# A softcap-attention and soft-MoE kernel on one core: one vector operation moved behind the norm in chunk 53, and matrix products without use put into two waits of TensorE

## The chip, the cores and the metric

The kernel runs on one core of a Trainium2 chip. The metric is the device time of one execution in microseconds (us). The core has five engines that run side by side, each with its own queue in program order: TensorE (PE in the profile, with its weight loads listed apart as PEld), VectorE (DVE), ScalarE (ACT), GpSimd (POOL) and SyncE (SP, which here only starts transfers). An engine waits on semaphores that other engines or transfers raise.

## The reference

Attention over 8 batches of 12 heads, 448 tokens of 64 values each, with capped scores, and then a soft mixture of experts over all 3584 tokens of 768 values, with 32 slots for 8 experts. Its core:

```python
scores = scale * q @ k.T;  scores = cap * tanh(scores / cap)
attn = softmax(scores);    x = (attn @ v)           # 3584 x 768
logits = x @ phi                                     # 3584 x 32
d = softmax(logits, over tokens); c = softmax(logits, over slots)
slot_input = d.T @ x                                 # 32 x 768
h = relu(slot_input[e] @ w1[e]); slot_out[e] = h @ w2[e]
out = c @ slot_out                                   # 3584 x 768, float32
```

## The kernel before, in words

**Tiles and chunks.** Heads are taken in 48 pairs, and the keys of a pair in 7 tiles, so there are 336 tiles of 128 x 448 scores. Six tiles are a chunk; there are 56 chunks (0 to 55). Two halves of a chunk have three tiles each. The main loop (lines 899 to 932) goes over the chunks j. In each round it issues, engine by engine in this order: the tanh of the chunk's two halves on ScalarE (`tanh_chunk`, line 354, its instructions are L361 and L365), the exponential of the chunk before on ScalarE (`exp_chunk`, line 375, L373), the product of finished exponentials with the values for the pair that ended two chunks ago (`pv_first`, line 654, `pv_tail`, line 667, `pv_rest`, line 671; the products are L634), and the scores of the next chunk (`qk_chunk`, line 337, L348).

**The exponential chain.** ScalarE does not take all exponentials. `SHARED` (line 381) gives VectorE the first 1 to 3 tiles of some chunks. `poly_exp` (line 603) computes them as a chain of seven operations, numbered 0 to 6 (L609, L611, L612, L613, L614, L615, L616); operations 2 to 5 work on two tiles of scratch, `xf` and `xp`, of which there is one each. The table `POLY` (line 382) says where in the round each operation of each chunk is issued: the key is a chunk and a slot, the slot's sign says whether it stands ahead of ("<") or behind (">") the other work of that slot.

**Slots.** `run(j, slot)` (line 866) issues the work that `at(j, slot, ...)` put there (line 795). Within a round the slots come in the order 0, m, e, a, b, r, c, d. Between slot b and slot c stands `pv_rest`, which ends with the norm.

**The norm.** `norm` (line 638) reads the sums of a pair from the PSUM tile `pv`, takes their reciprocal (L641) and multiplies (L644) into `xq`. There is one `pv` tile (pool `psV`, one buffer), so the next pair's first product waits until L644 has read it.

**Work around chunk 53.** In slot a of a round with a finished pair, `pv_first` writes `pv`; slot c of chunk 53 has `slot_sums` of batch 6 (line 778; L769, L775 and L727 on TensorE, L785 on VectorE). GpSimd copies values into `vbd` (`vcast`, line 285, L288) when the products that read it have ended.

**Products without use.** `busy` (line 878, L882 and L885) multiplies ones into a bank that nobody reads; `spare` (line 800) does it in the `pv` bank; `fill` (line 660, L664) multiplies ones into 57 unused columns of the last `pv` tile. `FILL` (line 804) and `LATE` (line 860) say where. In chunk 34 slot b has `e_transp` of batch 3 (line 730, L739), and slot c a `spare`.

**The start.** `first_half(0)` (line 240) prepares the first pair: casts, transposes on TensorE (L236), and copies (L238). The list at lines 249 to 255 is the order of its pieces. The transposes of key tiles 3 to 6 go into the bank `three`, a part of the tile `boots[1]`, and wait for GpSimd's cast of those keys (L232) and for ScalarE's copy out of `three`.

**After the chunks.** The last pairs are finished (`TAILSEQ`, line 999), the slot inputs are summed, and the two layers of the experts run on TensorE (L1078, L1106). Some parts of w2 come back from a scratch tensor by 21 transfers that SyncE starts as attention's memory is given back (L1057). Then output tiles are made and stored (L1134).

Of the kernel before, what the change touches and what calls it, by code (L numbers as in the profile page):

```python
# [20 lines left out]
NT = 7  # L21
# [3 lines left out]
CS = 3  # L25
# [12 lines left out]
def kernel(  # L38
# [31 lines left out]
    pe, dve, act, pool, sp = nc.tensor, nc.vector, nc.scalar, nc.gpsimd, nc.sync  # L70
# [111 lines left out]
    def load(nm, Q):  # L182
        if Q < NQ:
            t = raw_tile(nm)
            pool.dma_start(out=t, in_=quad_ap(nm, Q))  # L185
            raws[nm, Q] = t
# [37 lines left out]
    def first_pieces(h, jobs):  # L224

        for stage, nm, c0, c1, eng, bank, at0 in jobs:
            copy = act.copy if eng is act else pool.tensor_copy if eng is pool else dve.tensor_copy
            cols = slice(h * HP, h * HP + HP)
            if stage == "junk":
                busy(c0)  # L230
            elif stage == "cast":
                copy(casts[nm, 0][:, c0:c1, cols],  # L232
                     raws[nm, 0][h][:, c0 * DH:c1 * DH].rearrange("p (c d) -> p c d", d=DH))
            elif stage == "turn":
                for c in range(c0, c1):
                    pe.transpose(bank[cols, at0 + c - c0, :], casts[nm, 0][:, c, cols], ident)  # L236
            else:
                copy(qkT[nm, 0][cols, c0:c1, :], bank[cols, at0:at0 + c1 - c0, :])  # L238

    def first_half(h):  # L240
        for nm in ("k", "q"):
            if h == 0:
                qkT[nm, 0] = qk[0].tile([P, NT, P], BF16, name=nm + "T", tag=nm + "T")
        one = psT.tile([P, 8, P], BF16, name="ps1", tag="T")
        two = psV.tile([P, NT, P], BF16, name="ps2", tag="pv")
        if h == 0:

            three = boots[1][:, CS - 1, :].bitcast(BF16).rearrange("p (c q) -> p c q", q=P)
            first_pieces(h, (("cast", "q", 4, NT, act, None, 0), ("cast", "k", 0, CS, dve, None, 0),
                             ("cast", "q", 0, 4, dve, None, 0), ("turn", "q", 4, NT, pe, three, 0),  # L250
                             ("turn", "k", 0, CS, pe, two, 0), ("copy", "q", 4, NT, act, three, 0),
                             ("cast", "k", CS, NT, pool, None, 0),
                             ("turn", "q", 0, 4, pe, one, 0), ("copy", "k", 0, CS, dve, two, 0),
                             ("copy", "q", 0, 4, dve, one, 0), ("turn", "k", CS, NT, pe, three, 3),
                             ("copy", "k", CS, NT, dve, three, 3)))
        else:
            first_pieces(h, (("cast", "k", 0, NT, dve, None, 0), ("cast", "q", 0, NT, dve, None, 0),
                             ("turn", "k", 0, NT, pe, two, 0), ("turn", "q", 0, NT, pe, one, 0),
                             ("copy", "k", 0, NT, dve, two, 0), ("copy", "q", 0, NT, dve, one, 0)))
            for nm in ("q", "k"):  # L260
                raws.pop((nm, 0)), casts.pop((nm, 0))
                load(nm, 2)
# [112 lines left out]
    def exp_chunk(j):  # L375
# [201 lines left out]
            (53, 'm'): ((52, 2),),  # L577
            (53, 'e'): ((53, 0), (52, 3), (51, 6), (52, 4)),
            (53, '>a'): ((53, 1), (52, 5)),
            (53, '<b'): ((53, 2),),  # L580
            (53, '>d'): ((53, 3),),
            (54, 'm'): ((54, 0),),
            (54, 'e'): ((53, 4), (52, 6)),
# [211 lines left out]
    def at(j, slot, f, *a):  # L795
        if j < 0:
            j, slot = 0, "b"
        aux.setdefault((j, slot), []).append((f, a))
# [61 lines left out]
    LATE = ((52, 'd', 3, 1), (54, 'd', 3, 3),)  # L860
    for j, slot, n, parts in LATE:
        at(j, slot, spare, n, parts)
    for n in range(2):
        at(0, "c", vcast, 0, n)

# [10 lines left out]
    junk = boots[0][:, 0, 0:P]  # L876
# [11 lines left out]
    junk = boots[1][:, 0, 0:P]  # L888
    busy(27)
    first_half(0)  # L890
    qk_chunk(0)
    qk_chunk(1)
    spare(6)
    first_half(1)
    pool.dma_start(out=phib, in_=moe_phi.rearrange("(jt ji) s -> ji jt s", ji=P))

# [62 lines left out]
    junk = sl_ps[1][:, P:512]  # L959
# [220 lines left out]
    for n in range(B // 2 * NT):  # L1180
        bb, c = divmod(n, NT)
# [58 lines left out]
```

## Time and profile before

| what | us |
|---|---|
| three runs: median (lowest to highest) | 286.31 (284.74 to 288.71) |
| the profiled execution: device time | 283.64 |
| the profiled execution: span of its instructions | 281.9 |
| PE busy in the span | 245.5 (87%) |
| ACT busy | 249.2 (88%) |
| DVE busy | 240.0 (85%) |
| POOL busy | 141.4 (50%) |

Busy time is a union over the engine's instructions and says how full an engine is, not whether anything waits for it. The lines that are used are quoted where they are used. Times in the timeline and in the chain of waits are counted from the start of the span.

### The profile page before, as it was taken

How to read it: one execution, taken by the hardware profiler on the slowest of the kernel's cores; microseconds unless marked ns; L12 is line 12 of the kernel's file. 1: busy time of each engine (PE TensorE's matmuls, PEld its weight loads, DVE VectorE, ACT ScalarE, POOL GpSimd, SP SyncE). 2: the span in 40 equal slices, each digit the busy share in tenths (PEclk: the TensorE clock that was granted, in tenths of full speed). 3: DMA queues.
4: the chain of work that ended last, by engine and by line, in shares of the span. 5: the costliest groups of instructions: out<-in, count | busy, mean ns of one | idle time of the engine just before them, and what ended most of it. 6: DMA issues, size and time to landing. Idle time of an engine off the chain costs nothing.

```text
span 281.9 us, 10429 instructions
## 1 busy us (share of the span) xinstructions
PE 245.5 (87%) x4553; PEld 165.9 (59%) x4553; DVE 240.0 (85%) x474; ACT 249.2 (88%) x198; POOL 141.4 (50%) x198
## 2 busy tenths in 40 slices
PE   8898889998998999889989999899988989997720
PEld 6655556765675667566657675667566758642400
DVE  3479999999999999999999999999999996447840
ACT  4999999999999999999999999999999996236730
POOL 7986457653955385628663857295734210200000
PEclk9999999999999999999999999999999999999985
DMA  7999999999999999999999999999999579959997
GB/s 228 266 192 204 224 212 229 232 221 218 211 225 222 216 230 231 219 216 218 230 219 203 212 225 223 217 214 226 221 217 218 137 226 318 410 200 391 414 420 306
DMA packets 58332, 68.08 MB, mean 242 GB/s; under 512 B 4144, under 2 KB 54448, under 8 KB 58288
## 3 DMA queue, kind: packets, MB, share of 16 engines
q0 software_dynamic: 42448, 35.31, 79.5%
q1 hardware_dynamic: 15552, 31.89, 32.4%
q8 instruction: 35, 0.57, 0.7%
q10 hardware_dynamic: 288, 0.23, 0.2%
q14 instruction: 9, 0.07, 0.1%
HBM read 91.72 MB, written 19.27 MB: 394 GB/s over the span
## 4 chain that ended last, share of the span: by engine, by line
ACT 40%; PE 29%; DVE 20%; issue 4%; DMA 3%; POOL 1%; DVEq 0%; ACTq 0%; POOLq 0%
ACT ex L373 16%; ACT ex L365 15%; PE pv L634 8%; ACT ex L361 7%; PE sc L348 4%; DVE xq L644 3%; DVE xp L612 3%; PE so_ps L1106 2%; DVE xp L614 2%; PE hp L1078 2%; DVE xf L611 2%; DVE qT L280 2%; DVE ex L609 2%; DVE ex L615 2%; PE op L1146 1%
## 5 line engine op out<-in xcount | busy, mean ns | idle before, releaser
L365 ACT ACTIVATE ex<-sc 128x1344 f16<-128x1344 f32 (+1 forms) x91 | 118.2, 1400 | 1.3 <-PE sc L348 1.3
L373 ACT ACTIVATE ex<-ex 128x1344 bf16<-128x1344 f16 (+5 forms) x58 | 109.7, 1894 | 0.1
L634 PE MATMUL pv<-vbd,ex 128*128 128x130 bf16 (+1 forms) x1610 | 95.1, 212 | 10.2 <-POOL vbd L288 4.4
L634 PEld LDWEIGHTS <-ex 128*128 128x128 bf16 (+1 forms) x1680 | 75.6, 101 | 38.8 <-issue 6.2
L288 POOL CAST vbd<-vraw 64x896 bf16<-64x896 f32 x46 | 47.8, 1040 | 58.4 <-PE pv L634 40.1
L348 PE MATMUL sc<-qT,kT 64*64 64x448 bf16 x672 | 66.5, 359 | 5.3 <-ACT ex L365 3.7
L348 PEld LDWEIGHTS <-kT 64*64 64x64 bf16 x672 | 22.4, 105 | 14.4 <-ACT ex L365 6.3
L644 DVE TENSOR_TENSOR xq<-pv,rec 128x448 bf16<-128x448 f32 x46 | 28.7, 624 | 1.6
L361 ACT ACTIVATE ex<-sc 128x2688 f16<-128x2688 f32 x11 | 28.1, 2550 | 0.2 <-PE sc L348 0.2
L614 DVE TENSOR_TENSOR xp<-xp,xf 128x1344 f16<-128x1344 f16 (+2 forms) x34 | 27.4, 807 | 0.5
L612 DVE TENSOR_TENSOR xp<-xf 128x1344 f16<-128x1344 uint16 (+2 forms) x34 | 27.5, 809 | 0.2
L615 DVE TENSOR_TENSOR ex<-ex,xp 128x1344 uint16<-128x1344 uint16 (+2 forms) x34 | 26.9, 791 | 0.2
L116 POOL DMA_DIRECT2D w1b<-in_moe_w_dram x32 | 25.9, 810 | 0.0
L280 DVE COPY kT<-kps 128x896 bf16<-128x896 bf16 x23 | 14.2, 616 | 4.9 <-PE kps L275 2.8
L609 DVE TENSOR_SCALAR ex<-ex 128x1344 uint16<-128x1344 f16 (+2 forms) x34 | 17.0, 501 | 1.2 <-ACT ex L361 0.7
L296 POOL MEMSET vbd<- 64x1 bf16 x22 | 3.1, 139 | 29.3 <-PE pv L634 29.0
L613 DVE TENSOR_SCALAR xp<-xp 128x1344 f16<-128x1344 f16 (+2 forms) x34 | 17.2, 506 | 0.6
L611 DVE TENSOR_SCALAR xf<-ex 128x1344 uint16<-128x1344 uint16 (+2 forms) x34 | 17.1, 504 | 0.3
L185 POOL DMA_DIRECT2D qb<-in_q_dram x22 | 16.3, 740 | 1.8 <-PE qps L278 0.9
L616 DVE TENSOR_SCALAR ex<-ex 128x1344 uint16<-128x1344 uint16 (+2 forms) x34 | 16.1, 474 | 0.2
L185 POOL DMA_DIRECT2D kb<-in_k_dram x22 | 16.3, 741 | 0.0
L120 POOL DMA_DIRECT2D w2d<-in_moe_w_dram x21 | 16.1, 785 | 0.0
(124 smaller groups left out, 317.8 us busy)
## 6 DMA issues: line engine op xcount, KB each, us to landing
w1b<-in_moe_w_dram POOLq DMA_DIRECT2D x32, 384.0 KB, 9.8
vraw<-in_v_dram SPq DMA_DIRECT2D x44, 224.0 KB, 6.2
w2d<-in_moe_w_dram POOLq DMA_DIRECT2D x21, 384.0 KB, 9.0
w2t<-w2d SPq DMA_DIRECT2D x21, 384.0 KB, 7.4
out_dram<-ob SPq DMA_DIRECT2D x7, 768.0 KB, 6.9
qb<-in_q_dram POOLq DMA_DIRECT2D x22, 224.0 KB, 8.0
kb<-in_k_dram POOLq DMA_DIRECT2D x22, 224.0 KB, 7.7
w2b<-in_moe_w_dram POOLq DMA_DIRECT2D x11, 384.0 KB, 9.0
```

The lines of the kernel that those rows point to most:

```text
L116: pool.dma_start(out=w1b[e][:, js, fs], in_=w1r[:, e, js, fs])
L185: pool.dma_start(out=t, in_=quad_ap(nm, Q))
L288: pool.tensor_copy(vbds[Q % 2][r, :, :, c0:c0 + DH], raw[r])
L348: ins = pe.matmul(sc[cs, u, 0:S], qkT["k", Q][r, c, cs], qkT["q", Q][r, :, cs], start=True, stop=True).ins
L361: apart["t", i - 1] = apart["t", i] = act.activation(exs[j].bitcast(F16), own["board"][:, :, 0:S], ACT.Tanh, scale=qk_scale / cap).ins
L365: ins = act.activation(exs[j][:, half * CS + u0:half * CS + u1, :].bitcast(F16), (own[0] if i == u0 == 0 else sc)[:, u0:u1, 0:S], ACT.Tanh ...
L373: act.activation(exs[j][:, u0:u1, :], exs[j][:, u0:u1, :].bitcast(F16), ACT.Exp, scale=cap)
L612: lambda: dve.tensor_tensor(p, s, s.bitcast(F16), op=ALU.mult),
L614: lambda: dve.tensor_tensor(p, p, s, op=ALU.mult),
L615: lambda: dve.tensor_tensor(y, y, p, op=ALU.add),
L634: pe.matmul(out_, exs[j][r, u, q0:q0 + (HP if tail else P)], v_, start=(c == 0 and g == gs[0] < NF), stop=(c == NT - 1), skip_group_check= ...
L644: dve.tensor_tensor(xq[Q][:, h, s0:s1, :], pv[:, 0:s1 - s0, 0:DH], rec.to_broadcast([P, s1 - s0, DH]), op=ALU.mult)
```

## The change

Three edits, none of which changes a result.

First, in the pieces of the first pair, `busy(3)` (three products of 128 x 128 ones into columns of `boots[1]`) is put ahead of the transposes of key tiles 3 to 6. In the built program the first of the three waits for ScalarE's copy out of that tile; the transposes after them wait only for GpSimd's cast.

Second, operation 2 of chunk 53's exponential chain (L612 on 128 x 1344) goes from slot "<b" to slot "<c". In VectorE's queue it then stands behind the reciprocal L641 and the product L644 and ahead of L785; everything else on VectorE keeps its place.

Third, `fill(7)` (seven products of 57 columns) is put at the head of slot b in chunk 34. In TensorE's queue they stand behind the scores of that round and ahead of the transposes L739. The first of them waits for VectorE's norm of the last pair.

```diff
-                             ("copy", "q", 0, 4, dve, one, 0), ("turn", "k", CS, NT, pe, three, 3),
+                             ("copy", "q", 0, 4, dve, one, 0), ("junk", "k", 3, 0, pe, None, 0),
+                             ("turn", "k", CS, NT, pe, three, 3),
                              ("copy", "k", CS, NT, dve, three, 3)))
...
             (53, '>a'): ((53, 1), (52, 5)),
-            (53, '<b'): ((53, 2),),
+            (53, '<c'): ((53, 2),),
             (53, '>d'): ((53, 3),),
...
     for j, slot, n, parts in LATE:
         at(j, slot, spare, n, parts)
+    at(34, "<b", fill, 7)
```

Each of the two changed or added lines shifts the numbers of the lines behind it by one.

## The prediction

> **What bounds the kernel now.** I read four views in this order: the page's busy times, the windows with the granted clock, the chain of waits from 218 us on, and the timeline around each edit.
>
> ```profile
> PE 245.5 (87%) x4553; PEld 165.9 (59%) x4553; DVE 240.0 (85%) x474; ACT 249.2 (88%) x198; POOL 141.4 (50%) x198
> ACT  4999999999999999999999999999999996236730
> ```
> ```profile
> 225.00:230.00 5.00, 3.95 (x79) 2.88 (x76) 4.90 (x10) 4.83 (x5) 0.73 (x2) 1.00 0.60 187
> 254.00:256.00 2.00, 2.00 (x29) 0.57 (x28) 1.41 (x3) 1.42 (x3) 0.00 (x0) 1.00 1.05 393
> 270.00:275.00 5.00, 0.65 (x4) 0.19 (x2) 1.94 (x2) 0.90 (x1) 0.00 (x0) 0.80 1.02 422
> ```
>
> ScalarE is full from the second slice to about 235 us, so in the middle only what delays ScalarE counts. Near the end that changes: in the row of 225 to 230 us ScalarE and TensorE both have gaps (4.83 and 3.95 of 5). The third number from the right of a windows row is TensorE's granted clock: 1.00 in the rows up to 270, lower only in the last, where its work ends. From 254 us on the transfers are full (share 1.05). The chain of waits shows who holds the end:
>
> ```profile
> 224.75 1.60 DVE xp L612
> 226.35 0.13 DVE rec L641
> 226.48 0.02 issue
> 226.50 0.64 DVE xq L644
> ...
> 236.59 0.79 PE pvl L634 x12
> ```
>
> This is the place of the second edit. Up to 226.50 + 0.64 VectorE holds the end, with an operation of 1.60 us ahead of the norm; from then on TensorE does, by the products for `pv` that follow (of the chain's 28 pieces from there to 237.4 us, 27 are work of TensorE), up to the last products of attention, those at 236.59 among them. Time won at 227 us is won at the end, if nothing else steps in.
>
> **The moved operation.** The timeline of VectorE, GpSimd, TensorE and ScalarE there:
>
> ```profile
> 224.71 0.93 POOL L288 CAST vbd<-vraw 64x896 bf16<-64x896 f32 x1 [3.13 <-PE pv L634]
> 225.65 0.56 PE L348 MATMUL sc<-qT,kT 64*64 64x448 bf16 x6
> 226.27 0.19 DVE L641 RECIPROCAL rec<-pv 128x7 f32<-128x7 f32 x1
> 227.04 0.38 DVE L785 TENSOR_TENSOR slacc<-slps,slacc 128x224 f32<-128x224 f32 x1
> 227.27 0.84 PE L634 MATMUL pv<-vbd,ex 128*128 128x130 bf16 x12 [1.05 <-DVE xq L644]
> 227.34 0.50 DVE L613 TENSOR_SCALAR xp<-xp 128x1344 f16<-128x1344 f16 x1
> 227.47 1.55 ACT L373 ACTIVATE ex<-ex 128x1344 bf16<-128x1344 f16 x1
> 228.71 0.27 DVE L616 TENSOR_SCALAR ex<-ex 128x448 uint16<-128x448 uint16 x1
> 229.18 1.29 ACT L365 ACTIVATE ex<-sc 128x1344 f16<-128x1344 f32 x1 [0.17 <-PE sc L348]
> 230.01 0.21 DVE L641 RECIPROCAL rec<-pv 128x7 f32<-128x7 f32 x1
> 230.04 0.95 POOL L288 CAST vbd<-vraw 64x896 bf16<-64x896 f32 x1
> 230.25 0.62 DVE L644 TENSOR_TENSOR xq<-pv,rec 128x448 bf16<-128x448 f32 x1
> ```
> ```profile
> L612 DVE TENSOR_TENSOR xp<-xf x34: 385/848/1602, 14.0 to 231.7; 128x1344 f16<-128x1344 uint16 x27, 128x896 f16<-128x896 uint16 x5, 128x448 f16<-128x448 uint16 x2
> L644 DVE TENSOR_TENSOR xq<-pv,rec x46: 623/624/626, 21.9 to 234.1; 128x448 bf16<-128x448 f32 x46
> ```
>
> L612 takes 0.85 us in the median; the 1.60 is its longest, and it started at 224.75, just behind GpSimd's cast (224.71 to 225.64). The excess of 0.75 lies inside the cast. L644 never took over 0.626 us, the one at 230.25 beside the cast of 230.04 included.
>
> After the edit: the operation ahead of L612 is done by 224.75, and so are the products for `pv`, since the cast that waits for them too starts at 224.71. So L641 starts near 224.7 rather than 226.27, and L644 ends near 224.7 + 0.19 + 0.04 + 0.62 = 225.5 rather than 227.12. L612 follows near 225.45 and meets the last 0.2 us of the cast; with its usual 0.85 it ends between 226.30 and 226.50, about where it ended before. The norm is then free: its 0.81 us fills time that L612 lost waiting. L785 goes next; its sums are ready, since TensorE is at the scores behind them from 225.65. Before, L641 started at 226.27 and L785 at 227.04, 0.77 apart; this stretch drops out from behind L612, so L785 starts near 226.27 and L613 near 226.57 rather than 227.34. VectorE gains 0.77 us.
>
> ```profile
> 28.21 1.21 ACT ex L373
> ```
> ```profile
> 235.55 0.57 ACT L373 ACTIVATE ex<-ex 128x448 bf16<-128x448 f16 x1
> 251.92 10.99 SPq L1134 DMA_DIRECT2D out_dram<-obh  x19
> ```
> ```profile
> L1106 PE MATMUL so_ps<-w2t,hpad x84: 326/326/338, 248.7 to 255.9; 128*32 128x384 bf16 x84
> L1057 SPq DMA_DIRECT2D w2t<-w2d x21: 319/363/974, 222.6 to 243.6; - x21
> DMA to landing us min/median/max: 3.1/7.4/7.8
> ```
>
> What is late next, step by step. TensorE's 12 products need L644 (225.5) and the end of the scores before them (225.65 + 0.56 = 226.21), so they start near 226.2: 1.1 us earlier. `pv_rest` of that round needs L616 of chunk 52, which VectorE does at 228.71; it moves 0.77. The norm at 230.01 moves 0.77 to 0.8. ScalarE's tanh at 229.18 waited 0.17 for scores, and started 229.18 - 227.47 = 1.71 us behind the exponential before it, where the chain shows 1.21 for such a pair. So ScalarE moves 0.50 us. Its last exponential ends at 236.12 and TensorE's products that need it start at 236.59: with 0.50 and 0.77 the two become 235.62 and 235.82, still in order. If ScalarE moved only by its idle 0.17, they would be 235.95 and 235.82, and 0.64 is left of 0.77. The w2 transfers cannot eat it: the last is issued at 243.6, lands at most 7.8 later (251.4), and its products run just before 255.9. The stores start when output tiles exist (251.92) and fill the transfers from 254 on, so the whole store phase moves with its start. Sum of this edit: -0.77 us, between -1.1 (TensorE's own gain) and 0.
>
> One rule bears on it. The Trainium skill, "SBUF — State Buffer", section "SBUF: two separate sides", says that VectorE with two SBUF inputs and GpSimd take a shared port as an exclusive lock, held for a whole instruction. The trace agrees: L612 ended at 226.35, which is the cast's end (225.64) plus 0.71. The rule speaks against the full gain: the moved L612 meets the lock again, is held to 225.64, and with a whole 0.85 behind it ends at 226.49, which leaves 0.77 - 0.14 = 0.63; with the 0.71 that the row shows, it is 0.77, and I take that.
>
> **The products at the start.**
>
> ```profile
> 4.48 0.47 ACT L238 COPY qT<-boot 64x384 bf16<-64x384 bf16 x1 [0.44 <-PE boot L236]
> 5.29 0.41 PE L236 MATMUL boot<-ident,casts 128*64 128x128 bf16 x4 [0.40 <-POOL casts L232]
> 6.05 0.54 ACT L365 ACTIVATE ex<-sc 128x448 f16<-128x448 f32 x1 [1.10 <-PE sc L348]
> ```
> ```profile
> 1.16 2.74 PE L885 MATMUL boot<-ones 128*128 128x128 bf16 x27
> 9.84 1.07 PE L885 MATMUL junk<-ones 128*128 128x128 bf16 x16
> ```
>
> TensorE idles 0.40 us, from 4.89 to 5.29. The three products may start when the copy ends (4.48 + 0.47 = 4.95, and 0.04 for the signal). One costs (1.07 - 0.22) / 15 = 0.057 us as at 9.84, or 2.74 / 27 = 0.10 as at the start. Three end by 5.16 or 5.29: hidden under the wait for GpSimd's cast. The cover gone, they would cost 0.17 to 0.30 on the way to the first tanh at 6.05. I take 0; a gain is excluded in this trace, since the transposes wait for the cast.
>
> **The products in chunk 34.**
>
> ```profile
> 144.93 0.56 PE L348 MATMUL sc<-qT,kT 64*64 64x448 bf16 x6 [0.17 <-ACT ex L365]
> 145.35 0.61 DVE L696 COPY xT<-xps 128x896 bf16<-128x896 bf16 x1
> 146.01 0.49 PE L739 MATMUL eps<-ident,E 128*32 128x128 bf16 x16 [0.51 <-DVE xT L696]
> 149.21 0.83 PE L664 MATMUL pv<-ones 128*128 128x57 bf16 x25
> ```
>
> TensorE idles 0.51 us from 145.49 until VectorE's copy ends at 145.96. Seven products at 0.83 / 25 = 0.033 us are 0.23: hidden. The norm that the first waits for ended before that copy began on the same engine. Without cover they would cost 0.23; I take 0.
>
> **Sum.** -0.77 + 0 + 0 = -0.77 us: the profiled execution would go from 283.64 to 282.87 (span 281.9 to 281.1). That execution is 2.67 us below the median of the runs shown; carried to the median, 286.31 - 0.77 = 285.54, and I forecast 285.5.
>
> **Rivals.** First, ScalarE or the transfers hold the end. For it: ScalarE is full to 235 us and its slack behind TensorE is 0.2 us by the sum. Against it: its 0.50 of gain is in the rows. With the gain cut to 0 to 0.4 us: 286.1.
>
> Second, the products matter through the clock. The runs shown spread from 284.74 to 288.71, 4.0 us, and only one has a clock on record; in others TensorE's clock may have dropped, and the products would keep it up. Against it: the clock was 1.00 on both sides of the idle times they fill. If it holds, the runs come together near the undisturbed execution: 283.64 - 0.77 = 282.9. The Trainium skill, "TensorE: Matmul & The Clock Gate", section "Part 1: The HAM clock gate (the "warmup" mystery)", says that a free-running activity window of about 3.4 us sets the clock, so that its phase differs between runs; idle times of 0.4 and 0.5 us are far shorter, which by that rule makes the products worth nothing in most phases. The trace, one phase, cannot decide it.
>
> Third, on the other side: the moved work shifts TensorE's idle times and the clock falls between 229 and 250 us, where TensorE holds the end. The row at 270 us shows that it does fall (0.80, mixed of 1.00 and less) when TensorE idles. At half the clock for 3.5 us, 1.75 us of work is lost: 286.31 - 0.77 + 1.75 = 287.3. Against it: the row of 225 to 230 kept 1.00 with 1.05 us idle, and the edit removes that idle. It decides once more than 1.54 us are spent at half the clock (0.77 lost).
>
> Last, the edit does not do what it says: L612 meets the whole cast again behind the norm and VectorE gains nothing: 286.3. The cast starts before L641, so I count this with the first.
>
> **How the numbers follow.** Forecast (gain 0.5 to 1.1): 0.58, range of its own 285.2 to 285.8 before the spread of runs. First rival with the last: 0.18. Second: 0.12. Third: 0.12. Both sides are open and the runs scatter by 1.6 below and 2.4 above their median, so the range reaches to the second rival (282.9) and over the third (287.3) by part of that scatter: 282.9 to 287.9. Two per cent is 5.7 us, about what a measurement of this kernel can tell from no change; no case reaches 280.6 or 292.0 except through scatter: faster 0.05, same 0.89, slower 0.06.
>
> **What would show it.** Right: L612 of chunk 53 starts near 225.5 and takes about 0.9 to 1.1 us; TensorE's wait of 1.05 us for L644 ahead of `pv` is gone; ScalarE's 0.17 us at 229.18 is gone; the first store (251.92) stands about 0.8 us earlier; the first tanh stays at 6.05 and the transposes L739 follow the copy as before. Wrong: the chain of waits passes through ScalarE after 230 us, a clock below 1.00 before 270 us, or the first tanh later than 6.1 us.

## The result and the profile after

| | median, us | lowest to highest | executions |
|---|---|---|---|
| before, with 14 more runs | 284.06 | 283.39 to 288.71 | 17 |
| after | 282.86 | 281.90 to 283.70 | 17 |

The ratio of after to before is 0.9958, with a 95% interval of 0.9940 to 0.9976: about 1.2 us less, between 0.7 and 1.7. That is within 2 per cent, as forecast. The predicted time was 285.5 with a range from 282.9; the measured 282.86 lies just below that range. Of the three executions that the prediction saw, 288.71 was one of the disturbed ones that the comparison leaves out, and with 14 more the median of before came to stand 2.25 us lower.

The profiled execution of after took 283.45 us (span 281.7), only 0.19 us less than that of before. Its engines, and a cut of its chain of waits (start, duration, what):

```profile
PE 246.5 (88%) x4563; PEld 167.0 (59%) x4563; DVE 239.5 (85%) x474; ACT 249.1 (88%) x198; POOL 140.9 (50%) x198
```
```profile
223.87 0.56 PE sc L349 x5
224.44 0.83 PE pv L635 x15
225.27 0.55 PE slps L770 x18
225.81 0.29 PE slps L776 x12
226.11 0.29 PE slps L728 x4
226.40 0.49 PE sc L349 x6
226.89 0.79 PE pv L635 x12
```

Before, VectorE held this stretch: 1.60 us of L612, the reciprocal and the norm, and then TensorE's 12 products. Now VectorE is gone from the chain here and TensorE runs through. The windows say the same. Columns after the length are the busy times of PE, PEld, DVE, ACT and POOL, then the granted clock, the transfers' share and GB/s:

```profile
225.00:230.00 5.00, 5.00 (x107) 3.83 (x108) 4.93 (x14) 5.00 (x5) 1.41 (x3) 1.00 0.78 249
270.00:275.00 5.00, 0.56 (x4) 0.10 (x2) 1.94 (x2) 0.90 (x1) 0.00 (x0) 1.00 1.02 424
```

TensorE and ScalarE, which had 3.95 and 4.83 of these 5 us, have all 5. The clock is 1.00 in both rows.

The timeline of the place, in which line numbers are one higher (L613 is the moved operation):

```profile
224.58 0.51 DVE L612 TENSOR_SCALAR xf<-ex 128x1344 uint16<-128x1344 uint16 x1
...
225.33 0.21 DVE L642 RECIPROCAL rec<-pv 128x7 f32<-128x7 f32 x1
...
225.39 0.93 POOL L289 CAST vbd<-vraw 64x896 bf16<-64x896 f32 x1 [3.13 <-PE pv L635]
...
225.57 0.62 DVE L645 TENSOR_TENSOR xq<-pv,rec 128x448 bf16<-128x448 f32 x1
...
226.12 0.91 DVE L613 TENSOR_TENSOR xp<-xf 128x1344 f16<-128x1344 uint16 x1
...
226.83 0.86 PE L635 MATMUL pv<-vbd,ex 128*128 128x130 bf16 x12
...
227.25 0.50 DVE L614 TENSOR_SCALAR xp<-xp 128x1344 f16<-128x1344 f16 x1
...
228.62 0.27 DVE L617 TENSOR_SCALAR ex<-ex 128x448 uint16<-128x448 uint16 x1
...
228.64 0.90 PE L635 MATMUL pv<-vbd,ex 128*128 128x130 bf16 x15
...
229.35 1.50 ACT L366 ACTIVATE ex<-sc 128x1344 f16<-128x1344 f32 x1
...
229.76 0.19 DVE L642 RECIPROCAL rec<-pv 128x7 f32<-128x7 f32 x1
...
240.68 1.26 PE L1080 MATMUL hp<-w1b,slT 128*32 128x512 bf16 x20
```

Times must not be subtracted from those of before as they stand: this execution reached chunk 53 later. I count from an event ahead of the edit, the start of operation 1 of chunk 53 (L612 here, L611 in before), to the first product of the experts' first layer (L1080 here, L1078 in before). The rows of before, from its timeline:

```profile
223.90 0.51 DVE L611 TENSOR_SCALAR xf<-ex 128x1344 uint16<-128x1344 uint16 x1
...
229.07 0.90 PE L634 MATMUL pv<-vbd,ex 128*128 128x130 bf16 x15
...
240.87 1.05 PE L1078 MATMUL hp<-w1b,slT 128*32 128x512 bf16 x16
```

Before that is 240.87 - 223.90 = 16.97 us, after it is 240.68 - 224.58 = 16.10 us: 0.87 us less. I call it the stretch below.

### The profile page after: what moved, and what is told of

Same layout as the page of the kernel before. It is cut to its first block, busy times and chain, and to the rows that moved or that the text cites. A ratio compares the mean times of both kernels' runs of the same rounds, so it can differ in the third digit from the quotient of the medians.

```text
span 281.7 us, 10449 instructions
## 1 busy us (share of the span) xinstructions
PE 246.5 (88%) x4563; PEld 167.0 (59%) x4563; DVE 239.5 (85%) x474; ACT 249.1 (88%) x198; POOL 140.9 (50%) x198
## 4 chain that ended last, share of the span: by engine, by line
ACT 38%; PE 31%; DVE 20%; issue 5%; POOL 1%; DVEq 0%; ACTq 0%
ACT ex L374 16%; ACT ex L366 14%; PE pv L635 8%; ACT ex L362 7%; PE sc L349 4%; DVE xq L645 2%; DVE xp L615 2%; PE so_ps L1108 2%; PE hp L1080 2%; DVE xp L613 2%; DVE ex L616 2%; ACT ob L1202 2%; PE op L1193 1%; DVE xf L612 1%; PE op L1148 1%
## 5 line engine op out<-in xcount | busy, mean ns | idle before, releaser
L645 DVE TENSOR_TENSOR xq<-pv,rec 128x448 bf16<-128x448 f32 x46 | 28.7, 625 | 1.6
L615 DVE TENSOR_TENSOR xp<-xp,xf 128x1344 f16<-128x1344 f16 (+2 forms) x34 | 27.5, 808 | 0.5
L616 DVE TENSOR_TENSOR ex<-ex,xp 128x1344 uint16<-128x1344 uint16 (+2 forms) x34 | 26.9, 791 | 0.2
L613 DVE TENSOR_TENSOR xp<-xf 128x1344 f16<-128x1344 uint16 (+2 forms) x34 | 26.9, 790 | 0.2
L614 DVE TENSOR_SCALAR xp<-xp 128x1344 f16<-128x1344 f16 (+2 forms) x34 | 17.0, 500 | 0.6
L612 DVE TENSOR_SCALAR xf<-ex 128x1344 uint16<-128x1344 uint16 (+2 forms) x34 | 17.2, 507 | 0.3
L617 DVE TENSOR_SCALAR ex<-ex 128x1344 uint16<-128x1344 uint16 (+2 forms) x34 | 16.5, 484 | 0.2
```

The costliest lines, as they stand in the source:

```text
L613: lambda: dve.tensor_tensor(p, s, s.bitcast(F16), op=ALU.mult),
L615: lambda: dve.tensor_tensor(p, p, s, op=ALU.mult),
L616: lambda: dve.tensor_tensor(y, y, p, op=ALU.add),
L645: dve.tensor_tensor(xq[Q][:, h, s0:s1, :], pv[:, 0:s1 - s0, 0:DH], rec.to_broadcast([P, s1 - s0, DH]), op=ALU.mult)
```

## The experiments

The stretch was read in each trace, with the same two rows. "Ratio" is to runs of before taken beside the kernel's own, with its 95% interval. The medians of those runs of before went from 283.88 to 284.96 us, so medians of two kernels in this table are compared to no better than about 1 us; their stretches are.

| kernel | operation 1 | experts | stretch | median | ratio |
|---|---|---|---|---|---|
| before | 223.90 | 240.87 | 16.97 | | |
| after | 224.58 | 240.68 | 16.10 | 282.86 | 0.9958 (0.9940 to 0.9976) |
| second edit alone | 224.06 | 240.16 | 16.10 | 282.92 | 0.9949 (0.9928 to 0.9970) |
| first edit alone | 223.93 | 240.90 | 16.97 | 284.24 | 0.9986 (0.9955 to 1.0017) |
| third edit alone | 223.74 | 240.71 | 16.97 | 283.31 | 0.9983 (0.9945 to 1.0020) |
| no edit, cast behind operation 2 | 225.01 | 241.23 | 16.22 | 283.02 | 0.9958 (0.9927 to 0.9989) |
| operation 2 four times | 225.14 | 249.52 | 24.38 | 290.36 | 1.0209 (1.0143 to 1.0275) |
| second edit, some products removed | 224.25 | 240.86 | 16.61 | 283.71 | 0.9974 (0.9952 to 0.9997) |
| the same, cast behind L611 | 224.22 | 240.31 | 16.09 | 282.93 | 0.9945 (0.9917 to 0.9973) |
| 12 products at the start | 225.10 | 242.06 | 16.96 | 284.12 | 0.9983 (0.9956 to 1.0010) |
| 28 products in chunk 34 | 225.89 | 242.85 | 16.96 | 285.85 | 1.0040 (1.0008 to 1.0072) |
| 18 products behind the norm | 223.94 | 241.53 | 17.59 | 285.25 | 1.0037 (1.0012 to 1.0061) |
| 34 products in the wait | 223.97 | 240.94 | 16.97 | 284.28 | 1.0012 (0.9994 to 1.0031) |
| second and third edit | 224.05 | 240.15 | 16.10 | 282.46 | 0.9919 (0.9883 to 0.9956) |

**Second edit alone.**

```diff
-            (53, '<b'): ((53, 2),),
+            (53, '<c'): ((53, 2),),
```

> The second edit alone (operation 2 of chunk 53 behind the norm). Theory A, the moved operation carries the gain: 0.8 to 1.0 us below the kernel before (ratio 0.9965 to 0.9972), TensorE's wait of 1.05 us for L644 ahead of pv gone, the expert layer about 0.9 us nearer to the first tanh than before. Theory B, the products without use carry it: within 0.3 us of the kernel before (ratio 0.999 to 1.001).

Measured: 282.92 us, and a stretch of 16.10, the same as with the whole change. The moved operation carries the gain of the stretch. The ratio of 0.9949 is below the 0.9965 to 0.9972 expected of it; the interval reaches up to 0.9970.

**First edit alone, and with 12 products in place of 3.**

```diff
+                             ("junk", "k", 3, 0, pe, None, 0),
```

> The first edit alone (three products in the wait of the first pair). Theory A: no gain, between 0 and 0.3 us longer (ratio 1.000 to 1.001), since the three are hidden under the wait for the cast when TensorE's clock has risen before them, and cost 0.17 to 0.3 us when it rises later. Theory B, the products raise the clock earlier or hold it: 0.3 to 1.0 us shorter (ratio 0.9965 to 0.999).

> The first edit alone with twelve products instead of three. Theory A, they are hidden only as long as TensorE waits for the cast: twelve take 0.69 us at the full clock and 1.28 us at half, the wait covers about 0.3 us, so the first tanh comes 0.4 to 1.0 us later than with none and the time is 0.4 to 1.0 us above the kernel before (ratio 1.0015 to 1.0035). Theory B, activity at the start pays: no longer than the kernel before (ratio 1.000 or less).

Measured: 284.24 us with 3 products. With 12: 284.12 us. Neither can be told from no change: the 0.4 to 1.0 us that 12 were expected to cost do not show in the median, although in the trace the first tanh starts at 7.08 us. The traces do not agree on the start. In the first the transposes of key tiles 3 to 6 begin at 5.50 us, 0.21 later than in before, but so does GpSimd's cast that they wait for (5.05 against 4.84 us). What differs more between traces is TensorE's pace at this point. The trace of after, and below it that of the kernel with the cast behind operation 2, which has no products here:

```profile
4.52 0.95 PE L236 MATMUL ps<-ident,casts 128*64 128x128 bf16 x7
...
4.86 0.40 POOL L232 CAST casts<-kraw 128x256 bf16<-128x256 f32 x1 [0.59 <-DMA kraw<-in_k_dram]
...
5.41 0.34 PE L887 MATMUL boot<-ones 128*128 128x128 bf16 x3
...
5.68 0.41 PE L236 MATMUL boot<-ident,casts 128*64 128x128 bf16 x4
...
6.44 1.35 ACT L366 ACTIVATE ex<-sc 128x448 f16<-128x448 f32 x2 [1.20 <-PE sc L349]
```
```profile
4.49 0.95 PE L236 MATMUL ps<-ident,casts 128*64 128x128 bf16 x7
...
6.45 0.54 ACT L368 ACTIVATE ex<-sc 128x448 f16<-128x448 f32 x1 [1.24 <-PE sc L351]
```

Seven transposes took 0.95 us in both, where before's trace has 0.62, and the first tanh came at 6.44 and 6.45, with the products and without. In such an execution TensorE is late and the cast (done by 5.26) is no cover: the three products stand at 5.41 to 5.68, an exposed 0.27 us, although the first tanh came no later than in the kernel without them. In before's kind of execution they are hidden. The medians show no cost or gain of the first edit beyond their intervals.

**Third edit alone, and with 28 products in place of 7.**

```diff
+    at(34, "<b", fill, 7)
```

> The third edit alone (seven products in chunk 34). Theory A: no difference within 0.2 us (ratio 0.9993 to 1.0007), the products end before VectorE's copy does and the transposes start as before. Theory B, they hold the clock: 0.3 to 1.0 us shorter (ratio 0.9965 to 0.999), with a clock below 1.00 in chunk 34 of the kernel before to be seen in some execution.

> The third edit alone with 28 products instead of seven. Theory A, the wait for VectorE's copy covers 0.5 us and 28 take 0.16 + 28 x 0.027 = 0.9 us from the first start: the transposes start 0.2 to 0.4 us behind the copy's end, ScalarE's wait for the scores of the next chunk grows from 0.22 us to 0.4 to 0.6 us, and the time is 0.2 to 0.4 us above the kernel before (ratio 1.0007 to 1.0014). Theory B: no longer than the kernel before.

Measured: 283.31 us with 7, no difference; 285.85 us with 28, slower by 0.1 to 0.7 per cent. The timeline of TensorE in chunk 34, with 7 and then with 28:

```profile
144.82 0.57 PE L348 MATMUL sc<-qT,kT 64*64 64x448 bf16 x6 [0.23 <-ACT ex L365]
...
145.32 0.36 PE L664 MATMUL pv<-ones 128*128 128x57 bf16 x7
...
145.84 0.49 PE L739 MATMUL eps<-ident,E 128*32 128x128 bf16 x16 [0.16 <-DVE xT L696]
```
```profile
145.66 0.56 PE L348 MATMUL sc<-qT,kT 64*64 64x448 bf16 x6 [0.20 <-ACT ex L365]
...
146.16 0.92 PE L664 MATMUL pv<-ones 128*128 128x57 bf16 x28
...
147.01 0.49 PE L739 MATMUL eps<-ident,E 128*32 128x128 bf16 x16
```

From the scores to the transposes L739 it is 1.02 us with 7 (1.08 in before): they fill a wait that is there anyway. With 28 it is 1.35: the wait is used up and the rest, about 0.3 us, delays; the larger part of that kernel's 0.40 per cent (1.1 us) is not accounted for. So the 7 products show neither a cost nor a gain.

**No edit, but GpSimd's cast waits for operation 2.** The operation stays ahead of the norm as in before; only the lock is tested.

```diff
-        pool.tensor_copy(vbds[Q % 2][r, :, :, c0:c0 + DH], raw[r])
+        ins = pool.tensor_copy(vbds[Q % 2][r, :, :, c0:c0 + DH], raw[r]).ins
+        if "late" in apart:
+            tc.add_manual_dep(ins, apart.pop("late").name, ...)
...
-        steps[n]()
+        ins = steps[n]().ins
+        if (j, n) == (53, 2):
+            apart["late"] = ins
```

> Operation 2 of chunk 53 stays ahead of the norm as in the kernel before; instead GpSimd's cast into vbd that ran beside it waits until it has ended. Theory A1, the operation was long because the cast held it up: it takes 0.85 us instead of 1.60, the norm and VectorE's chain move by 0.75 us, and the time falls by 0.6 to 0.8 us (ratio 0.997 to 0.998). Theory A2, its length has nothing to do with the cast and only its place ahead of the norm costs: it stays near 1.6 us and the time is unchanged (ratio 0.999 to 1.001).

Measured: 283.02 us, stretch 16.22, 0.75 less than before. Its timeline (L615 is the operation):

```profile
225.85 0.86 DVE L615 TENSOR_TENSOR xp<-xf 128x1344 f16<-128x1344 uint16 x1
...
226.63 0.20 DVE L646 RECIPROCAL rec<-pv 128x7 f32<-128x7 f32 x1
...
226.93 0.93 POOL L288 CAST vbd<-vraw 64x896 bf16<-64x896 f32 x1 [4.25 <-DVE rec L646]
```

The operation took 0.86 us, against 1.60 in before, and only the cast had changed its place. So 0.74 us of it was the time that GpSimd's cast kept it waiting. Putting the norm ahead of the operation is a second way to get time back there, and it shortened the stretch by 0.12 us more (16.10).

**Operation 2 done four times ahead of the norm.** It asks what the opposite of the edit does, and whether a wait of TensorE's costs more than its length.

```diff
-            (53, '<b'): ((53, 2),),
+            (53, '<b'): ((53, 2),) * 4,
```

> The kernel before, with operation 2 of chunk 53 done four times instead of once ahead of the norm (the same result each time), so that TensorE's wait for L644 grows from 1.05 us to about 3.4 us. Theory A, the wait costs its own length and nothing else: 3 x 0.77 = 2.3 us longer than the kernel before, TensorE's granted clock 1.00 from the first rise to the end of its work. Theory C, so long a wait lowers TensorE's clock: 5 to 8 us longer, and the clock's record falls to 0.50 between 227 and 233 us.

Measured: 290.36 us in the median of only four executions (288.11 to 292.36; the traced one is the longest). The four together take 4.28 us, and TensorE waits 3.73 us for the norm. The windows of its trace:

```profile
224.00:228.70 4.70, 3.45 (x73) 2.28 (x70) 4.56 (x9) 4.70 (x5) 0.93 (x1) 1.00 0.90 301
228.80:242.40 13.60, 11.17 (x110) 8.22 (x111) 9.11 (x23) 8.50 (x8) 1.05 (x2) 0.50 0.38 131
242.50:250.00 7.50, 7.47 (x163) 5.97 (x164) 3.71 (x13) 1.31 (x4) 0.66 (x1) 1.00 0.99 348
```

TensorE's 12 products start at 231.18, behind the wait. The granted clock is 0.50 from within that wait for 13.6 us, long after they have come back. The stretch grew by 24.38 - 16.97 = 7.4 us for a wait that grew by 3.73 - 1.05 = 2.7. This is the third rival's mechanism, brought about by a longer wait; 1.05 us of idle time in before's trace left the clock at 1.00.

**Second edit, without the products of chunks 52 and 54.** It leaves out products without use only.

```diff
-            if (b or k > 2) and j + k < NCH - 1:
+            if (b or k > 2) and j + k < NCH - 2:
...
-    LATE = ((52, 'd', 3, 1), (54, 'd', 3, 3),)
+    LATE = ()
```

> The second edit alone, and besides it all products without use of chunks 52 and 54 taken out (three of 128 columns, eight of 57, one of 384), which stand on the chain behind the norm. Theory A, with the norm early TensorE is the bound there and these products cost their time: 0.29 + 0.21 + 0.28 us less than the second edit alone, at most 0.8 and at least 0.4, so 281.9 to 282.5 us. Theory C, they keep TensorE's clock up: the clock falls below 1.00 between 220 and 250 us and the time is 283.5 us or more.

Measured: 283.71 us, and a stretch of 16.61, 0.51 more than with them; the clock stayed at 1.00. Both theories missed: the products were not a cost to be saved, and it was not the clock. The timeline of chunk 54 names the cause:

```profile
229.00 1.07 POOL L288 CAST vbd<-vraw 64x896 bf16<-64x896 f32 x1
...
229.18 1.03 DVE L611 TENSOR_SCALAR xf<-ex 128x448 uint16<-128x448 uint16 x1
...
230.13 0.19 DVE L641 RECIPROCAL rec<-pv 128x7 f32<-128x7 f32 x1
```

L611 takes 0.27 us when alone. Without the products GpSimd's next cast began 0.18 us ahead of it and held it for 0.76; with them L611 had begun 0.04 us before that cast. The norm follows L611.

**The same, with that cast behind L611.** The dependency of the run above, set at `(54, 1)`.

> Edit 2 with the products of chunks 52 and 54 left out, as in the run without them, and GpSimd's cast of chunk 54 made to wait for VectorE's operation 1 of that chunk (L611). In the run without products that cast began at 229.00 us, 0.18 us before L611, and L611 took 1.03 us instead of 0.27; with the products L611 began 0.04 us before the cast. Theory 'lock': the 0.8 us that the run without products lost is L611 held by the cast; put in order, L611 takes 0.27 to 0.33, the norm behind it comes 0.7 to 0.8 us sooner and the time is that of edit 2 alone, 282.9 to 283.1. Theory 'products': the products themselves are worth the 0.8 us (through the clock or as cover); then the time stays at 283.6 to 283.8, ordered or not.

Measured: 282.93 us, stretch 16.09. All that the removed products seemed to be worth was which of two engines came first. Leaving them out gained nothing over the second edit alone (16.10) either: in both kernels the last products of attention wait for ScalarE, as the part on the prediction shows.

```profile
229.14 0.27 DVE L614 TENSOR_SCALAR xf<-ex 128x448 uint16<-128x448 uint16 x1
...
229.33 0.20 DVE L646 RECIPROCAL rec<-pv 128x7 f32<-128x7 f32 x1
...
229.53 0.95 POOL L288 CAST vbd<-vraw 64x896 bf16<-64x896 f32 x1 [0.62 <-DVE rec L646]
```

**No edit, and products into TensorE's wait of 1.05 us.** If idle time as such were the cost, filling it would help.

```diff
+    at(53, "d", fill, 18)
```

> The operation stays ahead of the norm as before; 18 products without use (0.05 us each, about 0.9 us) are put into the 1.05 us in which TensorE waits for that norm, behind the scores and ahead of the 12 products of probabilities with values. Theory A (the gain of edit 2 is VectorE's order and nothing else): TensorE's 12 products stay where they were relative to chunk 50 and the time is that of before, ratio 1.000 within 0.003. Theory C (what counts is that TensorE is not left idle there, since idle time lowers its clock later): the time falls as with edit 2, ratio 0.994 to 0.997, although the 12 products start no earlier.

Measured: 285.25 us. Neither theory was tested: the products write the buffer that the norm frees, so they ran behind it, at 227.22, and TensorE's 12 products started at 227.92, 0.61 us later than in before when counted from operation 1. It is a measure of the reverse instead: 0.61 us on this path makes the stretch 0.62 longer and the time 0.37 per cent longer. The next kernel writes unused columns of the scores' buffer:

```diff
+    def beside(n):
+        home = scores[max(scores)][:, CS - 1, S:512]
+        for _ in range(n):
+            pe.matmul(home, ones, ones[:, 0:512 - S], start=True, stop=True)
...
+    at(53, "d", beside, 34)
```

> The run before with products in this place (18 of them, behind the scores of chunk 53) wrote the buffer that the norm frees: its trace has them at 227.22 to 227.85 us, behind the norm, so that TensorE's wait stayed and the 12 products of probabilities with values came 0.65 us later. Here 34 products (0.026 us each, about 0.9 us) write unused columns of the scores' buffer and wait for nothing; the operation stays ahead of the norm as before. Theory A (the gain of edit 2 is VectorE's order and nothing else): TensorE's wait is filled, the 12 products stay where they were, and the time is that of before, ratio 1.000 within 0.003. Theory C (what counts is that TensorE is not idle there, since idle time lowers its clock later): ratio 0.994 to 0.997, as with edit 2, although nothing starts earlier. If the products delay what they stand ahead of: ratio 1.001 to 1.003, and the 12 products start later than 1.05 us behind the scores.

Measured: 284.28 us, and a stretch of 16.97, that of before to the hundredth. TensorE and ScalarE, two timelines of this kernel:

```profile
226.22 1.16 PE L671 MATMUL sc<-ones 128*128 128x64 bf16 x34
...
227.34 0.84 PE L634 MATMUL pv<-vbd,ex 128*128 128x130 bf16 x12
```
```profile
227.42 1.29 ACT L365 ACTIVATE ex<-sc 128x1344 f16<-128x1344 f32 x1 [0.74 <-PE sc L671]
...
229.82 1.28 ACT L365 ACTIVATE ex<-sc 128x1344 f16<-128x1344 f32 x1
...
234.12 2.63 ACT L373 ACTIVATE ex<-ex 128x1344 bf16<-128x1344 f16 x3
```

The wait is filled and nothing is gained: what counts is when the norm lets the products start. There is a second finding, which I had not planned. The tanh had to wait for the products in its buffer; the tanh at 229.18 in before comes at 229.82 here, and ScalarE's last exponentials start at 234.12 against 233.50, which is 0.55 us later when counted from operation 1. The stretch did not grow. So in the kernel before, at the end of attention, ScalarE has at least 0.55 us to spare.

**Second and third edit, without the first.**

> Edits 2 and 3 without edit 1. The three edits add up: edit 2 alone gave 0.9949, edit 3 alone 0.9983 with an interval across 1, so 282.3 to 283.0 (ratio 0.993 to 0.996), not to be told from edit 2 alone or from the whole change; if the 0.2 us that the three products at the start cost in the trace of edit 1 alone is real, 0.2 less than the whole change. If edit 3 has a gain of its own that edit 1 hides: 282.3 or below.

Measured: 282.46 us, the lowest median of all. Its interval overlaps that of the whole change, and 0.4 us between them is not settled.

## Why the prediction was right and wrong

*The failed step* is "carried to the median, 286.31 - 0.77 = 285.54": in it, the 2.67 us by which the profiled execution stood below the median of three runs. The sum took that distance as fixed. With 17 executions the median is 284.06, the distance is 0.42, and the same sum gives 283.29, against 282.86 measured. The range was built around 285.5, and its lower end was put at 282.9 for the second rival only, so that it ended where the sum for the profiled execution pointed.

That this sum, 283.64 - 0.77 = 282.87, meets the measured median is luck. It was a forecast for the profiled execution, and that of after took 283.45: it reached operation 1 of chunk 53 by 0.68 us later than before's (224.58 against 223.90), and 0.39 of that stands already at the first tanh (6.44 against 6.05). The median fell by 1.2 us and the stretch by 0.87; the 0.3 between them lies inside the interval, and no run shows a cause for it.

*The mechanism* was right as far as TensorE's 12 products, and not behind them. Counted from operation 1 of chunk 53 in each trace:

| step | predicted | measured |
|---|---|---|
| duration of operation 2 | 0.9 to 1.1 | 0.91 |
| TensorE's 12 products (227.27 to 226.83) | -1.1 | -1.12 |
| L613, now L614 (227.34 to 227.25) | -0.77 | -0.77 |
| ScalarE's tanh, start (229.18 to 229.35) | -0.50 | -0.51 |
| ScalarE's last exponential, end (236.12 to 236.50) | -0.50 | -0.30 |
| `pv_rest` (229.07 to 228.64) | -0.77 | -1.11 |
| the norm (230.01 to 229.76) | -0.77 to -0.80 | -0.93 |
| experts' first product | -0.77 | -0.87 |

*The path behind the 12 products* was wrong. The sum let VectorE's 0.77 set the end, by way of `pv_rest`, which was to wait for L616 of chunk 52. It does not at its start: after has it at 228.64 while that operation (L617 there) runs from 228.62 to 228.89. So it moved with TensorE by 1.11 us, and from there to the experts the chains of both kernels hold TensorE alone: neither VectorE nor the second norm set the end. The end gained 0.87 and not 1.11 because three groups of products on that chain took longer in after: 0.90 us instead of 0.84 at 231.06, 0.58 instead of 0.51 at 235.19, and 0.90 instead of 0.79 at 236.29, together 0.24. The third in after, and its fifth product in before:

```profile
235.71 0.79 ACT L374 ACTIVATE ex<-ex 128x448 bf16<-128x448 f16 x1
236.23 0.40 PE L635 MATMUL pvl<-vbd,ex 128*128 128x130 bf16 x4
236.56 0.35 PE L635 MATMUL pvl<-vbd,ex 128*128 128x130 bf16 x3
```
```profile
236.76 0.39 PE L634 MATMUL pvl<-vbd,ex 128*128 128x130 bf16 x4
```

Four products start between 236.23 and 236.41. The fifth is the first that reads the last key tile (`TAILSEQ`); it starts at 236.56, 0.06 us behind the end of ScalarE's last exponential (236.50). In before that exponential ended at 236.12, 0.64 us ahead of the fifth product, which did not wait. The second group waits in the same way for the first of ScalarE's last three exponentials (ended 235.20), and the first group, by less, for VectorE's L617 (ended 231.56). ScalarE's own gain was also smaller than the sum had it: its tanh started 0.51 earlier, but took 1.50 us instead of the 1.29 that it took behind its wait, so that the ends, the last exponential's too, moved by only 0.30. So the end was set by ScalarE and not by VectorE, and 0.87 is near 0.77 by luck. The kernels with the second edit alone, with the second and third, and with the cast behind L611 have the same wait: the last exponential ends 11.92 to 11.93 us behind operation 1, the fifth product starts 0.06 later, and the stretch is 16.09 or 16.10. Where only the cast was moved there is no such wait, and the stretch gained VectorE's 0.75.

*The weighing of the lock* (0.63 by the rule, 0.77 by the row) came out for the row. The operation met the last 0.20 us of the cast (226.12 to 226.32) and ended at 227.03, which is the cast's end plus 0.71, as in before: part of its own time runs while it is held.

*The first rival*, that ScalarE or the transfers hold the end, came true in part: ScalarE held back about 0.2 of TensorE's 1.11 us. The kernel with 34 products shows that ScalarE had 0.55 us to spare in before, and the second edit used that up. The chain of waits of after does not name ScalarE there, since it books these short waits as time of the products. *The second* fell as to its cause: neither edit with products alone shows a change, and 34 products in the wait bring nothing. Yet the executions did come together as it forecast, by the second edit: alone it gave 282.56 to 283.40 us, the whole change 281.90 to 283.70, where the first edit alone gave 282.96 to 288.23 and the third alone 282.50 to 287.76. Why that is so stays open, since no trace was kept of one of the long executions. *The third* did not occur: the clock is 1.00 from the first 10 us to 275 us in the trace of after; in the kernel with a wait of 3.73 us it fell. *The last* (the lock met again) took 0.06 of the operation's 0.85 us.

*The first edit* at zero: right within the interval, but its cover is not always there; after's own trace has its 0.27 us exposed, and its first tanh at 6.44, which by my own test ("later than 6.1 us") would have counted against it. That test was no good, since a kernel without the edit shows 6.45. *The third edit* at zero was right within the interval.

What stays open besides: from the experts' first product to the first store the executions take between 10.35 us (third edit alone, 240.71 to 251.06) and 11.15 (after, 240.68 to 251.83; before 11.05). In after the chain shows 0.47 us of "issue" at 249.62, in before 0.37 at 250.14, and the kernel with the third edit alone has none in its row at 248.51 (36 products without a gap). No experiment was made on it.

## What to carry to other kernels

When a vector operation takes about twice its median in one place, look for a GpSimd instruction that began just ahead of it: the profile books the wait as busy time, so no idle time points to it. Here both ways out gave the time back: other work ahead of the held operation, and the GpSimd instruction made to wait. What such an edit is worth is read from an event ahead of the edit to an event behind it within each trace; here that gave -0.87 us to the hundredth in three kernels, where medians of 12 runs have intervals of 1 us. An engine with time to spare before an edit may have none behind it: ScalarE's 0.55 us were used up, and it set what the edit could gain. A chain of waits can miss this, so look for a gap inside a group of products. And the base of a forecast in absolute microseconds is not a median of three runs that spread by more than the effect.

## What the runs showed of the hardware

- A lead of 0.04 or 0.18 us decides a loss of 0.76: L611 took 0.27 us when it began 0.04 us before GpSimd's cast, and 1.03 when the cast began 0.18 us before it. Removing work on TensorE was enough to tip it, since that work set when the cast was released.
- The reciprocal and the product of the norm, which read PSUM, are not held: L645 took 0.62 us inside the cast of 225.39, as everywhere.
- In a wait of 3.73 us TensorE's recorded clock fell to 0.50 between 228.70 and 228.80, 1.3 us after its work ran out at 227.44, and stayed there for 13.6 us, 11.2 of them after work came back at 231.18. The Trainium skill, "TensorE: Matmul & The Clock Gate", section "Part 1: The HAM clock gate (the "warmup" mystery)", puts the fall after at least one idle window of about 3.4 us and the return after about one busy window. Neither agrees with this trace: the fall came sooner and the return later.
- The same seven transposes at the start took 0.55 to 0.62 us in ten traces and 0.95 in four, of kernels that are equal up to there.
